# Loads on one queue: a cap on the kilobytes that are underway before the next load is issued

## The chip, the cores and the metric

The kernel runs on one core of one Trainium2 chip. The time is the device time of one execution in microseconds. A core has five engines that run side by side and wait for one another through semaphores: TensorE (PE, with its weight loads shown apart as PEld), VectorE (DVE), ScalarE (ACT), GpSimd (POOL) and SyncE (SP). SP computes nothing here; it issues the DMA transfers between the chip's main memory and the on-chip buffers, one after the other, and 16 DMA engines carry them out.

## The reference

The program is an attention block followed by a gated feed-forward block with a short convolution, over 8 batches of 576 positions, 8 heads of width 64, model width 512 and inner width 1024, all in float32.

```python
scores = scale * np.matmul(q, k.transpose(0, 1, 3, 2))
rel = pos[:, None] - pos[None, :]
mask_plain = (rel >= 0) & (rel < window)                                  # window 32, heads 0 to 3
mask_dil = (rel >= 0) & (rel < window * dilation) & (rel % dilation == 0) # dilation 4, heads 4 to 7
attn = softmax(where(mask, scores, -1e9)); x = attn @ v
...
h = np.maximum(x @ w_in, 0.0)
conv_out = sum over k in 0..2 of conv_w[k] * h shifted by k - 1           # along the sequence
gate = 1.0 / (1.0 + np.exp(-conv_out))
return (h * gate @ w_out)
```

The weights `w_in`, `w_out` and `conv_w` arrive in 64-bit floating point. Every query sees 32 keys, so the attention part needs only narrow bands of the score matrix.

## The kernel before

**Attention.** The work goes batch by batch. A batch has four head pairs: pairs 0 and 1 use the plain window ("p"), pairs 2 and 3 the dilated one ("d"). For each pair SP loads one tile `qk` with queries and keys (592 KB for p, 672 KB for d, line 324) and one tile `v` (384 KB, line 326). There are two `qk` buffers and three `v` buffers, used in turn. PE multiplies queries by keys in blocks of 32 by 64 (L352; where the mask is added by PE, L339 comes first), DVE and ACT do the softmax (L378 to L412), PE multiplies by the values (L423), and ACT and DVE split the result into a high part `xa` (L480) and a rest `xb` (L483), since the products that follow are done on two such parts to keep float32 precision.

**Weights.** A function `weights` loads a slice of `w_in` or `w_out` as 64-bit words (L626) and turns it into a high and a low float32 part, with one ACT step first (L635) and four or more DVE steps after it (L637 to L643, L666, L670); some slices are finished by PE and ACT (L655 to L664). The four `w_in` slices of 1024 KB land in the space that will hold the gates later (`g0early` to `g3early`). The `w_out` slices pass through one buffer `raw`, in two halves of 512 KB where the slice is in `HALVED`.

**Feed-forward.** PE computes x times `w_in` (L549 for the first two batches, L511 later), ACT takes the positive part, DVE and ACT do the convolution and the gate (L563 to L581), PE multiplies by `w_out` (L593), and the result is copied (L605) and stored by SP (L608).

**Order.** A planner class adds every piece of work as a task with an engine, a cost and a due time, walks through them by its own estimate of times, and writes each engine's instructions in the order found. The order is fixed when the program is built; at run time each engine takes its instructions in that order and waits on semaphores where data or a buffer is not ready. The planner also puts matmuls without a use (L707) into PE's gaps in the first part of the program. All loads and nearly all stores stand in one list on SP, so a load that waits holds up all that stand behind it. In that list a load waits for its buffer to come free (for `qk` and `v`, PE's last use of it) and for the transfer that used the same semaphore before it; there are eight such semaphores for DMA, taken in turn, and nothing else limits how many loads are underway.

Of the kernel before, what the change touches and what calls it, by code (L numbers as in the profile page):

```python
# [11 lines left out]
I32 = mybir.dt.int32  # L12
# [7 lines left out]
NP = 4  # L20
NB = 18
W = 64
NV = 6
# [72 lines left out]
class Buffer:  # L96


    def __init__(self, pool, spare=0):

        self.pool, self.spare, self.left, self.end, self.t = pool, spare, 0, 0.0, None


class Task:
    def __init__(self, engine, cost, due, run, after, uses, table):
        self.engine, self.cost, self.due, self.run, self.table = engine, cost, due, run, table
        self.after, self.uses, self.end = [t for t in after if t is not None], list(uses), None
        for b in self.uses:
            b.left += 1


class Planner:
# [110 lines left out]
def attn_moe(ctx: ExitStack, tc: tile.TileContext, qk_p, qk_d, v_p, v_d, w_in, w_out, conv, mask, out):  # L223
    nc = tc.nc
# [25 lines left out]
    plan = Planner()  # L250
# [46 lines left out]
    def queries(p, qk, hd, n):  # L297
# [8 lines left out]
        q0 = 512 + g * 48  # L306
        return [(qk[:, q0 + 16 * i:q0 + 16 * i + 32], key(2 * g + i, 4)) for i in range(2)]

    xs, scored = {}, []

    heads = {}

    def head(b, p, behind=None):


        due = PAIR[b][p]
        kind = p // 2
        qk, v, s = (Buffer(n) for n in ("qk", "v", "s"))
        early = NP * b + p in EARLY or behind is not None
        sc = [Buffer(n) for n in (("mm", "mm", "nn") if early else ("att",))]  # L320
        eased = NP * b + p in EASED
        held = lambda: sorted(s.t for s in sc[:2]) + [sc[2].t] if early else (0, 1, 2)
        n = (S + KP, QD + KD)[kind]
        lq = plan.add("SP", n * 0.00124, 3e3 + NP * b + p if behind else due - EXTRA[32], lambda: nc.sync.dma_start(
            out=qk.t[:, :n], in_=(qk_p, qk_d)[kind][b, p % 2]), uses=[qk])
        lv = plan.add("SP", 0.95, 3e3 + NP * b + p if behind else due - EXTRA[33], lambda: nc.sync.dma_start(
            out=v.t, in_=(v_p, v_d)[kind][b, p % 2]), uses=[v])

        def scores():
            at = held()  # L330
            if eased:

                own = ((0, 1), (2, 3)), ((2, 4),), ((1, 1),)
                if kind == 1:
                    own = ((3, 1), (2, 3)), ((3, 1), (2, 3)), ((4, 1),)
                for bank, runs in enumerate(own):
                    c = 0
                    for i, n in runs:
                        nc.tensor.matmul(banks[:, at[bank], c * W:(c + n) * W].rearrange("p (a k) -> p a k", k=W), ones,  # L339
                                         kinds_sb[:, i, :].unsqueeze(1).to_broadcast([128, n, W]),  # L340
                                         start=c == 0, stop=True, skip_group_check=True)
                        c += n
            order = [4 * t + i for i in range(4) for t in range(4)] + [16, 17]
            if kind == 0:
                order = [a + i for i in range(5) for a, end in RUNS if a + i < end]
            for n in order:
                for hd in range(2):
                    slot, quad = place(p, hd, n)
                    bank, c = (0, slot) if slot < 4 else (2, 0) if slot == 4 else (1, slot - 5)
                    parts = queries(p, qk.t, hd, n)  # L350
                    for i, (q, k) in enumerate(parts):
                        nc.tensor.matmul(banks[quad * 32:quad * 32 + 32, at[bank], c * W:c * W + W], q, k,  # L352
                                         start=i == 0 and not eased, stop=i == len(parts) - 1, skip_group_check=True)

        needs, due = behind or ([], due)
        last = plan.add("PE", (0.71, 0.86)[kind] + (0.5 if eased else 0.0), due, scores, [lq, made, kinds, *needs], [qk, *sc, s], "S")
        if NP * b + p in EARLY and b < 2:
            scored.append(last)
        heads[b, p] = last, lv, v, s, sc, held
# [252 lines left out]
    def weights(src, n, due, pair, summed=False, words=None, halved=False):  # L612

        f = n / 512
        hi, lo = pair
        raw = words or (Buffer("raw") if n > 512 else None)
        r, w = [Buffer("r")] if summed else [], [] if summed or n < 512 else [Buffer("w")]
        u = lambda d=F32: (hi.before if n > 512 else hi).bitcast(d)
        t = lambda d=F32: (w[0].t if w else lo.before if n > 512 else lo).bitcast(d)
        pairs = lambda: (raw[0].t.before if words else raw[0].t if raw else conv_raw)[:, :2 * n].bitcast(I32).rearrange("p (n t) -> p n t", t=2)  # L620
        raw, last = [raw] if raw else [], []
        for at in [slice(0, n // 2), slice(n // 2, n)] if halved else [slice(0, n)]:
            both = lambda at=at: pairs()[:, at]
            low, high = (lambda i=i, both=both: both()[:, :, i] for i in range(2))
            f = (at.stop - at.start) / 512
            part = plan.add("SP", 1.27 * f, due - EXTRA[34], lambda both=both, at=at: nc.sync.dma_start(  # L626
                out=both(), in_=src[:, at].bitcast(I32).rearrange("p (n t) -> p n t", t=2)), uses=raw)

            def step(cost, uses, run, after):
                return plan.add("DVE", 0.16 + cost * f, due + EXTRA[21], run, [after], uses)  # L630

            part = plan.add("ACT", 0.16 + 0.5 * f, due + EXTRA[20], lambda at=at, high=high: nc.scalar.activation(  # L635
                out=u()[:, at], in_=high().bitcast(F32), func=AF.Abs, scale=2.0 ** -112), [part], raw)
            part = step(0.265, [], lambda at=at: nc.vector.tensor_scalar(  # L637
                out=u(I32)[:, at], in0=u(I32)[:, at], scalar1=3, scalar2=None, op0=ALU.logical_shift_left), part)
            part = step(0.53, [*raw, *w], lambda at=at, high=high: nc.vector.scalar_tensor_tensor(  # L639
                out=t(I32)[:, at], in0=high(), scalar=-0x80000000, in1=u(I32)[:, at], op0=ALU.bitwise_and, op1=ALU.bitwise_or), part)  # L640
            part = step(0.265, w, lambda at=at: nc.vector.tensor_scalar(
                out=u(I32)[:, at], in0=t(I32)[:, at], scalar1=-0x800000, scalar2=None, op0=ALU.bitwise_and), part)
            last.append(step(0.53, [*raw, *r], lambda at=at, low=low: nc.vector.scalar_tensor_tensor(  # L643
                out=(r[0].t if summed else u())[:, at], in0=low().bitcast(U32), scalar=-2.0 ** -52 if summed else 2.0 ** -52,
                in1=u()[:, at], op0=ALU.mult, op1=ALU.mult), part))
        f = n / 512

        def step(cost, uses, run):
            return plan.add("DVE", 0.16 + cost * f, due + EXTRA[21], run, list(last), uses)

        if summed:
            part = plan.add("ACT", 0.16 + 0.465 * f, due + EXTRA[22], lambda: nc.scalar.copy(out=hi[:, :], in_=t()), last)

            def add(ps, at):
                nc.tensor.matmul(bank(ps), ident, t()[:, at], start=True, stop=False)  # L655
                nc.tensor.matmul(bank(ps), minus, r[0].t[:, at], start=False, stop=False)
                nc.tensor.matmul(bank(ps), minus, hi[:, at], start=False, stop=True)

            halves, added = [slice(0, 512), slice(512, 1024)], []
            pss = [Buffer("nn" if words else "mm") for _ in halves]  # L660
            for at, ps in zip(halves, pss):
                added.append(plan.add("PE", 1.43, due + EXTRA[23], lambda at=at, ps=ps: add(ps, at), [part, whole, negated], [*r, ps], "E"))

            return [plan.add("ACT", 0.6, due + EXTRA[24], lambda at=at, ps=ps: nc.scalar.copy(out=lo[:, at], in_=bank(ps)), added, [ps])  # L664
                    for at, ps in zip(halves, pss)]
        last = [step(0.53, w, lambda: nc.vector.tensor_tensor(out=t(), in0=t(), in1=u(), op=ALU.add))]  # L666
        if n < 512:
            return last[0]
        last = [plan.add("ACT", 0.16 + 0.465 * f, due + EXTRA[22], lambda: nc.scalar.copy(out=hi[:, :], in_=t()), last, w)]
        return [step(0.53, w, lambda: nc.vector.tensor_tensor(out=lo[:, :], in0=t(), in1=hi[:, :].bitcast(F32), op=ALU.subtract))] * 2  # L670
# [129 lines left out]
```

## Time and profile before

| what | value |
| --- | --- |
| median of 3 runs | 522.52 us (522.17 to 525.08) |
| the profiled execution's own time | 521.72 us |
| its span in the trace | 519.8 us |
| PE busy | 501.5 us (96%) |
| DVE busy | 392.0 us (75%) |
| ACT busy | 289.9 us (56%) |
| chain that ended last | PE 86%, DVE 6%, DMA 3%, issue 2%, ACT 2% |
| bytes on the loads' and stores' queue q1 | 51.10 MB |

The span is what the trace covers; some 1.9 us of the execution lie outside it. The page gives each engine's busy time, the granted TensorE clock and the share of the 16 DMA engines in slices of the span. "Issue" stands for time in which an engine waited for nothing that the profile shows. A row of the timeline has the start in us, the duration, the engine, the line, what was written from what, and in brackets how long the engine stood idle before and what released it. A row on a DMA issue gives the tile, the size, and the time from the issue to the landing of the last byte. The queue q8, of kind "instruction", brings program code: 58 packets and 0.95 MB in all.

### The profile page before, as it was taken

To read this page: it belongs to the slowest core of one execution; us is meant where nothing else is said; L and a number is where in the kernel's file an instruction comes from. 1 tells how busy PE (TensorE), PEld (TensorE's weight loads), DVE (VectorE), ACT (ScalarE), POOL (GpSimd) and SP (SyncE) were. 2 spreads that over 40 slices of the span, in tenths; PEclk is the share of its full clock that TensorE was granted. 3 is DMA by queue.
4 is the path that set the end of the run, shared out by engine and by line. 5 is a ranking of instruction groups with operands and counts; after the bars stand their busy time and mean duration, and the time that the engine had idled before them with its cause. 6 is when DMAs were issued, how large, how long until landed. Compare 5 with 4: busy or idle time off the path is not lost.

```text
span 519.8 us, 16579 instructions
## 1 busy us (share of the span) xinstructions
PE 501.5 (96%) x7416; PEld 438.5 (84%) x7416; DVE 392.0 (75%) x654; ACT 289.9 (56%) x648; POOL 2.0 (0%) x34
## 2 busy tenths in 40 slices
PE   7869999999999899999999999999999999999996
PEld 4547889998888699998888899998788899998885
DVE  3798999999999778799987759887685339982400
ACT  5785788757832258784342248875261258772410
POOL 1000000000000000000000000000000000000000
PEclk9998999999999999999999999999999999999999
DMA  8994551201546610005444700004431100001111
GB/s 290 340 365 149 152 173 54 83 0 42 184 157 212 200 45 0 1 0 184 146 150 137 238 31 1 0 2 135 156 99 45 43 21 0 1 1 42 40 53 50
DMA packets 16695, 52.29 MB, mean 101 GB/s; under 512 B 2032, under 2 KB 2416, under 8 KB 16112
## 3 DMA queue, kind: packets, MB, share of 16 engines
q1 hardware_dynamic: 16480, 51.10, 28.8%
q8 instruction: 58, 0.95, 0.8%
q10 hardware_dynamic: 144, 0.13, 0.1%
q14 instruction: 13, 0.11, 0.1%
HBM read 41.79 MB, written 9.44 MB: 99 GB/s over the span
## 4 chain that ended last, share of the span: by engine, by line
PE 86%; DVE 6%; DMA 3%; issue 2%; ACT 2%; SPq 0%; DVEq 0%; ACTq 0%
PE banks L593 38%; PE banks L511 29%; PE banks L549 6%; PE banks L423 6%; PE banks L352 5%; DMA qk<-in_qk_d_dram 2%; DVE u L563 1%; PE banks L707 1%; DMA qk<-in_qk_p_dram 1%; PE banks L655 1%; ACT s L389 1%; DVE m L378 0%; DVE w L639 0%; DVE x3b L483 0%; DVE r L643 0%
## 5 line engine op out<-in xcount | busy, mean ns | idle before, releaser
L593 PE MATMUL banks<-wo,g 128*128 128x512 f32 x864 | 204.2, 393 | 0.3 <-issue 0.3
L593 PEld LDWEIGHTS banks<-wo,g 128*128 128x128 f32 x864 | 160.3, 188 | 33.6 <-issue 0.5
L563 DVE SCALAR_TENSOR_TENSOR u<-u,conv_sb,u 128x576 f32<-128x576 f32 x104 | 84.3, 817 | 25.6 <-ACT u L569 24.5
L605 ACT COPY u<-banks 128x512 f32<-128x512 f32 (+1 forms) x36 | 20.9, 580 | 81.2 <-PE banks L593 79.8
L524 ACT ACTIVATE u<-banks 128x192 f32<-128x192 f32 (+1 forms) x96 | 36.8, 408 | 27.1 <-PE banks L511 24.8
L511 PE MATMUL banks<-x1a,wi 128*128 128x384 f32 x144 | 48.3, 335 | 0.0
L511 PE MATMUL banks<-x2a,wi 128*128 128x384 f32 x144 | 48.1, 334 | 0.0
L511 PE MATMUL banks<-x0a,wi 128*128 128x384 f32 x144 | 48.0, 335 | 0.0
L511 PE MATMUL banks<-x3a,wi 128*128 128x384 f32 x144 | 48.0, 335 | 0.0
L423 PE MATMUL banks<-pt,v 32*64 32x64 f32 (+2 forms) x2752 | 39.1, 227 | 6.9 <-issue 5.6
L423 PEld LDWEIGHTS banks<-pt,v 32*64 32x64 f32 x2752 | 35.1, 131 | 12.3 <-issue 7.4
L576 DVE TENSOR_TENSOR u<-u,u 128x576 f32<-128x576 f32 x52 | 38.9, 757 | 4.6 <-ACT u L574 4.1
L569 ACT ACTIVATE u<-u,conv_sb 128x576 f32<-128x576 f32 x52 | 40.6, 783 | 0.7
L352 PEld LDWEIGHTS banks<-qk 64*32 64x32 f32 x2432 | 28.7, 105 | 14.3 <-issue 9.0
L574 ACT ACTIVATE u<-u 128x576 f32<-128x576 f32 x52 | 35.1, 683 | 9.5 <-DVE u L563 8.8
L581 DVE TENSOR_TENSOR g<-u,g 128x576 fp32r<-128x576 f32 x52 | 38.3, 753 | 1.9 <-ACT g L579 1.7
L352 PE MATMUL banks<-qk 64*32 64x64 f32 x2432 | 34.5, 224 | 3.9 <-DMA qk<-in_qk_d_dram 1.6
L579 ACT CAST g<-u 128x576 fp32r<-128x576 f32 x52 | 34.5, 680 | 5.2 <-DVE u L576 5.1
L403 ACT ACTIVATE s<-s 128x576 f32<-128x576 f32 x23 | 15.8, 686 | 27.6 <-DVE s L401 27.4
L389 ACT ACTIVATE s<-banks,m 128x64 f32<-128x64 f32 x81 | 24.1, 330 | 6.6 <-DVE m L382 6.6
L511 PEld LDWEIGHTS banks<-x0a,wi 128*128 128x128 f32 x144 | 27.0, 188 | 0.1
L511 PEld LDWEIGHTS banks<-x1a,wi 128*128 128x128 f32 x144 | 27.0, 188 | 0.0
(155 smaller groups left out, 807.8 us busy)
## 6 DMA issues: line engine op xcount, KB each, us to landing
qk<-in_qk_d_dram SPq DMA_DIRECT2D x16, 672.0 KB, 5.1
qk<-in_qk_p_dram SPq DMA_DIRECT2D x16, 592.0 KB, 4.1
out_dram<-u SPq DMA_DIRECT2D x31, 256.0 KB, 2.2
v<-in_v_p_dram SPq DMA_DIRECT2D x16, 384.0 KB, 4.3
v<-in_v_d_dram SPq DMA_DIRECT2D x16, 384.0 KB, 4.7
raw<-in_w_out_dram SPq DMA_DIRECT2D x6, 512.0 KB, 6.8
out_dram<-u SPq DMA_DIRECT2D x9, 128.0 KB, 2.3
g0early<-in_w_in_dram SPq DMA_DIRECT2D x1, 1024.0 KB, 9.5
```

The costliest lines, as they stand in the source:

```text
L352: nc.tensor.matmul(banks[quad * 32:quad * 32 + 32, at[bank], c * W:c * W + W], q, k, start=i == 0 and not eased, stop=i == len(parts) - 1, ...
L423: nc.tensor.matmul(banks[hd * 64:hd * 64 + 64, bank, o:o + n], v.t[quad * 32:quad * 32 + 32, block // 2, block % 2 * 64:block % 2 * 64 + 6 ...
L511: nc.tensor.matmul(out if piece < 2 else out.rearrange("p (a n) -> p a n", a=2), wi[jw][fc // 2][:, fc % 2 * 512 + k * 128:fc % 2 * 512 + ...
L524: lambda h=h, ps=ps, n=n, to=to, at=at: nc.scalar.activation(out=h.t[:, to:to + n], in_=bank(ps)[:, at:at + n], func=AF.Relu), [last], [ps ...
L549: nc.tensor.matmul(bank(ps)[:, 0:HALF], wi[jw][fc // 2][:, fc % 2 * 512 + k * 128:fc % 2 * 512 + k * 128 + 128], x[k].t[jx][:, b % 2, hf * ...
L563: nc.vector.scalar_tensor_tensor(out=body(c[fc]), in0=h[fc].t[:, k:S + k], scalar=conv_sb[:, k, fc:fc + 1], in1=body(c[fc]), op0=ALU.mult, ...
L569: t = plan.add("ACT", 0.777, d, lambda fc=fc: nc.scalar.activation(out=body(c[fc]), in_=body(h[fc]), func=AF.Copy, scale=conv_sb[:, 1, fc: ...
L574: t = plan.add("ACT", 0.686, d + shaped, lambda fc=fc: nc.scalar.activation(out=body(c[fc]), in_=body(c[fc]), func=AF.Sigmoid), [t], [c[fc ...
L576: t = plan.add("DVE", 0.755, d + times, lambda fc=fc: nc.vector.tensor_tensor(out=body(c[fc]), in0=body(c[fc]), in1=body(h[fc]), op=ALU.mu ...
L579: hi = plan.add("ACT", 0.675, d + split, lambda fc=fc: nc.scalar.copy(out=gate(fc, 0), in_=body(c[fc])), [t, *(read[b - 1, fc] if b % 2 el ...
L581: lo = plan.add("DVE", 0.755, d + rest, lambda fc=fc: nc.vector.tensor_tensor(out=gate(fc, 1), in0=body(c[fc]), in1=gate(fc, 0).bitcast(F3 ...
L593: nc.tensor.matmul(bank(ps), g[k].t[:, k % 2, jg, col:col + 128], wo[jw][k // 2][:, k % 2 * 512:k % 2 * 512 + 512], start=(k == 0 and i == ...
```

## The change

Each load of `qk`, `v` and the weights now goes through one helper. It keeps a list of the loads issued so far that are not known to have landed, with their kilobytes. Before it issues a load it drops loads from the front of the list until those left hold at most 1,050 KB, and makes the new load wait for the landing of the last one dropped. The very first load of the masks, and all stores, stay outside the helper. The tasks, their costs, due times and order are the same. The sizes it counts are 592 or 672 KB for `qk`, 384 KB for `v`, 1024 or 512 KB for a weight slice or its half, and 24 KB for the convolution's weights.

```diff
--- before.py
+++ after.py
@@ -107,6 +107,9 @@
         self.after, self.uses, self.end = [t for t in after if t is not None], list(uses), None
         for b in self.uses:
             b.left += 1
+
+
+AHEAD = 1050
 
 
 class Planner:
@@ -306,6 +309,18 @@
         q0 = 512 + g * 48
         return [(qk[:, q0 + 16 * i:q0 + 16 * i + 32], key(2 * g + i, 4)) for i in range(2)]
 
+    underway = []
+
+    def load(to, what, kb):
+
+        it, behind = nc.sync.dma_start(out=to, in_=what), None
+        while sum(k for k, _ in underway) > AHEAD:
+            behind = underway.pop(0)[1]
+        if behind is not None:
+            tc.add_manual_dep(it.ins, behind.ins.name, mybir.DependencyInfo(mybir.DependencyClass.Sync, mybir.DependencyReason.DATA),
+                              reason="few loads underway")
+        underway.append((kb, it))
+
     xs, scored = {}, []
 
     heads = {}
@@ -321,10 +336,10 @@
         eased = NP * b + p in EASED
         held = lambda: sorted(s.t for s in sc[:2]) + [sc[2].t] if early else (0, 1, 2)
         n = (S + KP, QD + KD)[kind]
-        lq = plan.add("SP", n * 0.00124, 3e3 + NP * b + p if behind else due - EXTRA[32], lambda: nc.sync.dma_start(
-            out=qk.t[:, :n], in_=(qk_p, qk_d)[kind][b, p % 2]), uses=[qk])
-        lv = plan.add("SP", 0.95, 3e3 + NP * b + p if behind else due - EXTRA[33], lambda: nc.sync.dma_start(
-            out=v.t, in_=(v_p, v_d)[kind][b, p % 2]), uses=[v])
+        lq = plan.add("SP", n * 0.00124, 3e3 + NP * b + p if behind else due - EXTRA[32], lambda: load(
+            qk.t[:, :n], (qk_p, qk_d)[kind][b, p % 2], n // 2), uses=[qk])
+        lv = plan.add("SP", 0.95, 3e3 + NP * b + p if behind else due - EXTRA[33], lambda: load(
+            v.t, (v_p, v_d)[kind][b, p % 2], NV * 64), uses=[v])
 
         def scores():
             at = held()
@@ -623,8 +638,8 @@
             both = lambda at=at: pairs()[:, at]
             low, high = (lambda i=i, both=both: both()[:, :, i] for i in range(2))
             f = (at.stop - at.start) / 512
-            part = plan.add("SP", 1.27 * f, due - EXTRA[34], lambda both=both, at=at: nc.sync.dma_start(
-                out=both(), in_=src[:, at].bitcast(I32).rearrange("p (n t) -> p n t", t=2)), uses=raw)
+            part = plan.add("SP", 1.27 * f, due - EXTRA[34], lambda both=both, at=at: load(
+                both(), src[:, at].bitcast(I32).rearrange("p (n t) -> p n t", t=2), at.stop - at.start), uses=raw)
 
             def step(cost, uses, run, after):
                 return plan.add("DVE", 0.16 + cost * f, due + EXTRA[21], run, [after], uses)
```

On PE, DVE, ACT and POOL the instructions and their waits are the same as before. On SP the order is the same too; what differs is what a load waits for. A name such as DMAHW3_49 is one of the eight DMA semaphores, and it stands for the landing of the last transfer that used it. They are taken in turn by all transfers on SP: the masks have DMAHW0, the convolution's weights DMAHW1, the first `qk` DMAHW2, and so on.

The first place is the start of SP's list, from the first `v` (DMAHW3) to the second of two halves of a `w_out` slice. Before:

```order
L326 DMA v_90<-in_v_p_dram 128x768
L324 DMA qk_89<-in_qk_d_dram 128x1344
L626 DMA g0early<-in_w_in_dram 128x2048
L324 DMA qk_88<-in_qk_d_dram 128x1344 [waits DMAHW2_49,PE_49]
L626 DMA raw_131<-in_w_out_dram 128x1024
L324 DMA qk_89<-in_qk_d_dram 128x1344 [waits DMAHW4_49,DMAHW0_49,PE_49]
L626 DMA raw_131<-in_w_out_dram 128x1024 [waits DMAHW1_49]
```

And now:

```order
L316 DMA v_90<-in_v_p_dram 128x768
L316 DMA qk_89<-in_qk_d_dram 128x1344
L316 DMA g0early<-in_w_in_dram 128x2048 [waits DMAHW3_49]
L316 DMA qk_88<-in_qk_d_dram 128x1344 [waits DMAHW4_49,DMAHW2_49,PE_49]
L316 DMA raw_131<-in_w_out_dram 128x1024 [waits DMAHW5_49]
L316 DMA qk_89<-in_qk_d_dram 128x1344 [waits DMAHW6_49,DMAHW0_49,PE_49]
L316 DMA raw_131<-in_w_out_dram 128x1024 [waits DMAHW7_49,DMAHW1_49]
```

Nothing moved; `g0early` now waits for the first `v`, the `qk` behind it for the `qk` ahead of it, and each later load here for the one two places ahead.

The second place is some ten loads on, on the same engine, where two `w_in` slices follow each other (`g1early` whole, `g2early` in halves) and the third is near. Before:

```order
L626 DMA g1early<-in_w_in_dram 128x2048
L626 DMA g2early<-in_w_in_dram 128x1024 [waits DMAHW7_49]
L626 DMA g2early<-in_w_in_dram 128x1024 [waits DMAHW0_49]
L324 DMA qk_89<-in_qk_p_dram 128x1184 [waits DMAHW1_49,PE_49]
L326 DMA v_91<-in_v_p_dram 128x768 [waits DMAHW2_49,PE_49]
L626 DMA g3early<-in_w_in_dram 128x2048 [waits DMAHW3_49]
```

And now:

```order
L316 DMA g1early<-in_w_in_dram 128x2048 [waits DMAHW3_49]
L316 DMA g2early<-in_w_in_dram 128x1024 [waits DMAHW5_49]
L316 DMA g2early<-in_w_in_dram 128x1024 [waits DMAHW6_49]
L316 DMA qk_89<-in_qk_p_dram 128x1184 [waits PE_49]
L316 DMA v_91<-in_v_p_dram 128x768 [waits DMAHW0_49,PE_49]
L316 DMA g3early<-in_w_in_dram 128x2048
```

Here `g1early` has taken DMAHW6, so the second half of `g2early` waits for `g1early` to have landed, and the `v` ahead of `g3early` for that second half. Before, these loads waited for transfers that lay eight places back.

## The prediction

> **What bounds the kernel now.** I read the page's head first, then the busy times by stretch (columns: the stretch, its length, busy time and count for PE, PEld, DVE, ACT and POOL, PE's granted clock, DMA share, GB/s).
>
> ```profile
> span 519.8 us, 16579 instructions
> PE 501.5 (96%) x7416; PEld 438.5 (84%) x7416; DVE 392.0 (75%) x654; ACT 289.9 (56%) x648; POOL 2.0 (0%) x34
> 5.00:10.00 5.00, 3.44 (x150) 2.28 (x149) 0.99 (x3) 1.87 (x14) 0.00 (x0) 1.00 0.98 370
> 10.00:15.00 5.00, 4.19 (x129) 2.51 (x112) 3.94 (x9) 3.36 (x18) 0.00 (x0) 1.00 1.01 409
> 35.00:40.00 5.00, 2.35 (x89) 1.85 (x90) 3.47 (x7) 2.65 (x17) 0.00 (x0) 0.89 0.92 330
> 40.00:45.00 5.00, 5.00 (x96) 3.25 (x95) 3.89 (x7) 3.41 (x6) 0.00 (x0) 0.77 0.36 119
> 86.00:516.00 430.00, 426.82 (x5661) 381.22 (x5661) 321.08 (x517) 227.30 (x429) 0.00 (x0) 1.00 0.23 77
> ```
>
> From 86 us on PE is busy 426.8 of 430 us at full clock, while the DMA engines are used 23%. There a load can cost or save little. In the first 40 us it is the other way round: the DMA engines are full (share 0.92 to 1.01) and PE idles (2.35 of 5 us at 35 to 40). So a change to loads is worth what it moves the end of this opening; the rest follows as it stands.
>
> The chain of waits in the opening (start, duration, what):
>
> ```profile
> 7.03 7.19 DMA qk<-in_qk_d_dram
> 14.26 1.13 PE banks L352 x66
> ...
> 18.54 1.38 issue
> ...
> 35.97 2.00 issue
> 37.97 1.30 PE banks L423 x61
> ```
>
> PE waits for a `qk` to 14.22, and stands twice for nothing but "issue", 1.38 and 2.00 us, inside a run of value matmuls. What ends these two? The DMA view of 17.4 to 17.5 and of 35.5 to 35.6 shows one packet each on the instruction queue:
>
> ```profile
> q8 instruction: 1, 0.02, 69.1%
> ```
>
> ```profile
> q8 instruction: 1, 0.02, 61.3%
> ```
>
> PE goes on at 19.92 and 37.97, 2.5 and 2.4 us after them: twice the same distance. So I read them as PE short of code. The page has 58 such packets for 7,416 matmuls and as many weight loads, 256 instructions a packet. PE's waits for "issue" in 0 to 46 us (total, times, longest), and the count of packets:
>
> ```profile
> PE banks L423 <- issue: 3.4, 2, 2.0
> PE banks L352 <- issue: 0.6, 1, 0.6
> q8 instruction: 7, 0.11, 1.0%
> ```
>
> and in 86 to 516 us:
>
> ```profile
> PE banks L423 <- issue: 2.2, 2, 1.5
> PE banks L352 <- issue: 0.5, 1, 0.5
> PE banks L593 <- issue: 0.3, 1, 0.3
> q8 instruction: 44, 0.72, 0.7%
> ```
>
> That is 4.0 us for 7 packets beside full DMA engines, 0.57 each, against 3.0 for 44, 0.07 each. Longer matmuls explain part of the difference, for they use up code more slowly; crowded DMA engines may explain the rest.
>
> **The change, term by term.** No instruction is added to PE, DVE or ACT. SP gains waits, and behind each stand all later loads, though no store in the opening. To see when loads land now, I take the time from issue to landing of loads that ran alone (in order: at 45, 98.7, 48.6, 85 and 67.6 us):
>
> ```profile
> v<-in_v_p_dram SPq DMA_DIRECT2D x1, 384.0 KB, 3.4
> raw<-in_w_out_dram SPq DMA_DIRECT2D x1, 512.0 KB, 3.5
> qk<-in_qk_p_dram SPq DMA_DIRECT2D x1, 592.0 KB, 3.8
> qk<-in_qk_d_dram SPq DMA_DIRECT2D x1, 672.0 KB, 4.4
> raw<-in_w_out_dram SPq DMA_DIRECT2D x1, 1024.0 KB, 4.8
> ```
>
> Full engines move 409 GB/s (the row at 10 to 15), so 2.56 us for 1,024 KB. A load then lands at the later of two times: its issue plus its time alone, or the landing ahead of it plus its share of 2.56 us. The start, as issued and as it landed among others:
>
> ```profile
> 2.11 0.43 SPq L326 DMA_DIRECT2D v<-in_v_p_dram  x1
> 2.58 0.43 SPq L324 DMA_DIRECT2D qk<-in_qk_d_dram  x1
> g0early<-in_w_in_dram SPq DMA_DIRECT2D x1, 1024.0 KB, 9.5
> qk<-in_qk_d_dram SPq DMA_DIRECT2D x1, 672.0 KB, 6.7
> v<-in_v_p_dram SPq DMA_DIRECT2D x1, 384.0 KB, 4.8
> ```
>
> The `v` lands at 6.9 (2.11 + 4.8), and `g0early`, which was issued at about 3.06 (9.5 before it landed, just ahead of 12.57), waits for that. The `qk` between them lands at 8.6 (6.9 + 1.68, alone) to 9.3 (2.58 + 6.7, as before). Then, issue and landing: `g0early` 6.95, 11.8; `qk` 9.0, 13.6; `raw` 11.85, 15.35; `qk` 13.65, 18.05; `raw` 15.4, 19.3; `v` 18.1, 21.5; `qk` 18.5, 23.0; `v` 19.4, 24.0; `v` 21.55, 25.0; `g1early` 23.05, 27.9; the halves of `g2early` 25.05, 29.2 and 27.95, 31.45. Further on the same way: `v` 31.5, 34.9; `g3early` 31.9, 37.5; `v` 37.55, 41.0; the last `raw` half 41.05, 44.55. Where these are used now:
>
> ```profile
> 12.57 1.13 ACT L635 ACTIVATE wi03early<-g0early 128x1024 f32<-128x1024 f32 x1 [1.64 <-DMA g0early<-in_w_in_dram]
> 28.77 1.22 ACT L635 ACTIVATE wi02early<-g1early 128x1024 f32<-128x1024 f32 x1
> 30.76 1.35 ACT L635 ACTIVATE wi00early<-g2early 128x512 f32<-128x512 f32 x2
> 33.59 0.70 ACT L480 CAST x2a<-banks 128x64 fp32r<-128x64 f32 x2 [0.32 <-PE banks L423]
> 34.77 0.68 DVE L483 TENSOR_TENSOR x2b<-banks,x2a 128x512 fp32r<-128x512 f32 x1
> 45.69 0.68 ACT L635 ACTIVATE wo02early<-raw 128x512 f32<-128x512 f32 x1
> 50.03 0.41 ACT L556 ACTIVATE u<-banks 128x288 f32<-128x288 f32 x1 [3.66 <-PE banks L549]
> ```
>
> *First term, the early loads.* `g0early` and the third `qk` come about 0.7 us sooner (11.8 for 12.55, 13.6 for the 14.22 of the chain), because nothing is queued behind them that shares the engines. Both are waited for, so ACT and PE start sooner by 0.6. But the second half of `g2early`, at 31.45, then holds ACT: 0.68 for its L635 (half of 1.35) and 1.16 for the step behind it (L652, from 32.11 to 33.27, where the 0.32 idle begins) put L480 at 33.29 instead of 33.59. So at most 0.3 reaches DVE at 34.77. I take -0.3; the other bound is 0 (the loads share the engines as before). A shorter first stall (1.38) would be stopped at the same place, so it is worth nothing more.
>
> *Second term, the stall at 35.97.* It is ended by the code packet, not by PE's own work, so what counts is how soon that packet gets through. The loads that stood before it, first and last of five:
>
> ```profile
> 27.37 0.47 SPq L626 DMA_DIRECT2D g3early<-in_w_in_dram  x1
> 34.49 0.37 SPq L626 DMA_DIRECT2D raw<-in_w_out_dram  x1
> ```
>
> With their sizes they are 1024 + 512 + 384 + 672 + 512 = 3,104 KB, of which `g3early` was nearly through. By the list above only the `v` of 31.5 and `g3early` are underway at 34, 1,408 KB. Nothing in this trace shows the packet's time with half the queue. Bounds are 0 (it comes no sooner) and -2.0 (the stall goes); I take the middle, -1.0, since the 0.57 against 0.07 us a packet says crowding matters, and since the packet ahead of it came late too and would now come sooner.
>
> *Third term, lateness behind.* Loads land up to 2.5 us later from 19 to 45 us. The last `raw`, 44.55, is in time for ACT at 45.69, though only just if ACT is 1 us sooner; ACT has 3.66 us idle behind that row, so I count 0. After 45 us loads are far enough apart that the wait is met when SP comes to it, but for a few that are wanted only much later: 0.
>
> Sum: 519.8 - 0.3 - 1.0 = 518.5 of span, 520.4 of execution (521.72 - 1.3). The median of the runs lies 0.8 above that execution, so 522.52 - 1.3 = **521.2 us**.
>
> **Rivals.**
>
> *Code comes no sooner* (chance 0.24). The stalls shrink only if packets on q8 wait behind queued loads. If the engines serve q8 in turn with q1, depth does not matter, and only the first term stays: 522.52 - 0.3 = 522.2. Against it are the 0.57 us a packet; for it, that value matmuls outran their code by 1.5 us in the late stretch too, where the DMA engines are used 23%. The Trainium skill, "DMA: Bandwidth & Descriptors", section on queues, rings and completion order, says that each DMA engine goes round the queue rows it has work for, a packet at a time; by that rule this rival holds. Our two packets beside full engines do not settle it.
>
> *The whole stall goes, and the clock stays up* (0.15). PE's gaps of 34 to 38 us are followed by a clock of 0.77 in 40 to 45, with PE busy throughout: 5 x 0.23 = 1.2 us lost. Without the stall both come back: -0.3 - 2.0 - 1.2 = -3.5, 519.0 us. DVE and ACT must follow: ACT idles 2.35 of 5 us and DVE 1.53 at 35 to 40, so they could.
>
> *The waits starve the engines* (0.16). Each hand-off (landing, wait, issue, first byte) leaves the DMA engines with little queued. If each costs 0.4 us more than my list, five follow one another up to `g2early`'s second half, which lands at 33.45. DVE's x2b follows ACT's L480, which follows that landing by 1.84; x2b itself comes 0.7 after L480's start, so at 35.99 instead of 34.77. That is +1.2, 523.7 us. It decides from a landing of 32.2 on; a loss of 0.5% needs 34.8.
>
> *The waits never bind* (0.02): each is met before SP comes to it, 522.5 us. Against it: `g0early` stood ready to issue at 3.06, 3.8 us ahead of the landing it must now wait for.
>
> **How the numbers follow.** The forecast has 0.43. I count as no change what is within 0.5% (2.6 us), about what a measurement of this kernel can tell. Its own range is 520.2 to 522.5 by the bounds of the second term. With the rivals at 519.0 and 523.7 on the two ends, 519.0 to 523.8 holds 8 in 10. Faster by over 0.5%, below 519.9: the third of the cases nearly whole, 0.13, and 0.08 of the forecast's where the clock recovers too: 0.21. Slower, above 525.1: the far end of the starving case and things unseen, 0.11. Within: 0.68.
>
> **What would show it.** `g0early` used by ACT near 11.9 and PE's third score block near 13.6 show the first term; the first later than 12.6 refutes it. An "issue" gap near 35 us of 1 us is the second term; 2 us is the first rival, none with the clock at 1.00 the second. ACT's wait for a half of `g2early` above 1 us is the starving case. PE's busy share from 86 us on must stay as it is; a new wait for a load there would make all of this wrong.

## The result: slower by 1.05%, and the profile after

| | before | changed |
| --- | --- | --- |
| median, timed side by side | 523.24 us (4 runs, 522.17 to 525.08) | 528.73 us (4 runs, 527.58 to 530.66) |
| ratio, with its 95% interval | | 1.0105 (1.0061 to 1.0149) |
| the profiled execution | 521.72 us, span 519.8 | 527.58 us, span 525.5 |

Executions that fell into a slower state of the chip are left out of the times here and below. The forecast was 521.2 us, with a range of 519.0 to 523.8. The changed kernel lies outside it, on the other side. The page's head and the busy times by stretch of the changed kernel (the same columns as in the prediction):

```profile
span 525.5 us, 16579 instructions
5.00:10.00 5.00, 3.84 (x165) 2.73 (x165) 1.28 (x4) 2.58 (x18) 0.00 (x0) 1.00 0.91 332
10.00:15.00 5.00, 2.88 (x17) 1.31 (x15) 2.86 (x8) 2.27 (x10) 0.00 (x0) 1.00 0.77 257
30.00:35.00 5.00, 1.29 (x73) 1.12 (x72) 2.47 (x4) 2.65 (x4) 0.00 (x0) 0.68 0.75 225
35.00:40.00 5.00, 3.84 (x139) 3.20 (x132) 3.55 (x7) 3.70 (x15) 0.00 (x0) 0.50 0.89 333
40.00:45.00 5.00, 5.00 (x79) 3.20 (x63) 4.92 (x9) 3.04 (x11) 0.00 (x0) 0.50 0.70 220
86.00:516.00 430.00, 426.88 (x5735) 381.72 (x5734) 325.53 (x523) 230.70 (x436) 0.00 (x0) 1.00 0.23 76
```

In the last row PE is as busy as before, to 0.06 us of 430. One ACT instruction at the end of the opening, before and changed, shows where the time went:

```profile
86.86 0.81 ACT L569 ACTIVATE u<-u,conv_sb 128x576 f32<-128x576 f32 x1
```

```profile
91.21 0.81 ACT L584 ACTIVATE u<-u,conv_sb 128x576 f32<-128x576 f32 x1
```

By then the changed kernel is 4.35 us behind, of the 5.7 us by which its span is longer. So most of the time went in the opening, as the prediction said it could only go there; where the other 1.3 us of this one execution went is not settled here. What differs is the DMA side of the opening: a share of 0.77 and 257 GB/s at 10 to 15 us, where it was 1.01 and 409. PE is busy 1.29 of 5 us at 30 to 35, and behind that its clock is 0.50 for ten microseconds.

The chain of waits in the changed kernel (start, duration, what):

```profile
8.84 6.26 DMA qk<-in_qk_d_dram
...
15.18 4.85 DMA qk<-in_qk_d_dram
...
20.43 5.12 DMA qk<-in_qk_p_dram
...
25.57 6.47 DMA g1early<-in_w_in_dram
...
32.05 4.22 DMA g2early<-in_w_in_dram
...
36.71 6.79 DMA g3early<-in_w_in_dram
...
49.05 3.60 DMA raw<-in_w_out_dram
```

Each of these is one load from its issue to its landing, and each landing is what the next waits for: 15.10, 20.03, 25.55, 32.04, 36.27, 43.50, and 52.65 for the last half of `raw`. SP and the loads have become the chain; no computing engine stands between. Before, two loads stood in it, to 14.2 us, and then none to 132 us; from 23 to 60 us it was mostly steps on DVE and ACT, with PE at 36 to 43:

```profile
1.64 4.32 DMA qk<-in_qk_p_dram
...
7.03 7.19 DMA qk<-in_qk_d_dram
...
25.89 2.47 ACT s L389 x16
...
33.64 1.22 DVE w L639
...
132.39 5.33 DMA qk<-in_qk_d_dram
```

Where ACT uses the loads in the changed kernel:

```profile
13.50 1.12 ACT L650 ACTIVATE wi03early<-g0early 128x1024 f32<-128x1024 f32 x1 [2.73 <-DMA g0early<-in_w_in_dram]
32.06 1.12 ACT L650 ACTIVATE wi02early<-g1early 128x1024 f32<-128x1024 f32 x1 [3.54 <-DMA g1early<-in_w_in_dram]
34.02 0.69 ACT L650 ACTIVATE wi00early<-g2early 128x512 f32<-128x512 f32 x1
36.30 0.69 ACT L650 ACTIVATE wi00early<-g2early 128x512 f32<-128x512 f32 x1 [1.59 <-DMA g2early<-in_w_in_dram]
52.67 0.68 ACT L650 ACTIVATE wo02early<-raw 128x512 f32<-128x512 f32 x1 [4.11 <-DMA raw<-in_w_out_dram]
```

These are the rows L635 of before, 15 lines further down. `g0early` is used 0.93 us later than before (13.50 for 12.57), `g1early` 3.29 later (32.06 for 28.77), the last `raw` 6.98 later (52.67 for 45.69). The idle times in brackets are waits for the DMA; of these loads only `g0early` had one before, 1.64 us. The wait of 3.54 for `g1early` passes on to PE, as its longest of the whole trace. Beside it the waits for "issue" (total, times, longest):

```profile
PE banks L354 <- ACT wi L679: 4.2, 1, 4.2
PE banks L438 <- issue: 2.1, 2, 1.5
PE banks L367 <- issue: 1.1, 2, 0.6
```

The same view of before, over its whole span, for "issue":

```profile
PE banks L423 <- issue: 5.6, 4, 2.0
PE banks L352 <- issue: 1.4, 3, 0.6
PE banks L593 <- issue: 0.3, 1, 0.3
```

So 7.3 us of "issue" became 3.2. The waits that the prediction hoped to shorten are shorter by 4.1 us, but nothing shows that any time was won by it: in the opening, where they went, PE now stands for loads and for the other engines instead.

The whole stretch from 5 to 45 us sums it up. Before, then changed:

```profile
5.00:45.00 40.00, 31.44 (x906) 20.20 (x904) 29.99 (x63) 27.17 (x114) 0.00 (x0) 0.96 0.88 328
```

```profile
5.00:45.00 40.00, 30.61 (x815) 19.95 (x814) 29.03 (x61) 25.41 (x113) 0.00 (x0) 0.83 0.82 279
```

328 GB/s fell to 279. That is 49 GB/s x 40 us = 1.96 MB less brought in. At 328 GB/s it takes 6.0 us to make up, which is near the 5.5 us lost, but the nearness is no rule: of the caps below, the same sum gives 4.6 us for the 3.6 lost at 1,500 KB, and 20 us for the 48 lost at 0.

### The profile page after: what moved, and what is told of

It is laid out like the page before. It is cut to its first block, busy times and chain, and to the rows that moved or that the text cites. A ratio compares the mean times of both kernels' runs of the same rounds, so it can differ in the third digit from the quotient of the medians.

```text
span 525.5 us, 16579 instructions
## 1 busy us (share of the span) xinstructions
PE 504.7 (96%) x7416; PEld 441.2 (84%) x7416; DVE 392.6 (75%) x654; ACT 289.7 (55%) x648; POOL 2.0 (0%) x34
## 4 chain that ended last, share of the span: by engine, by line
PE 84%; DMA 11%; DVE 2%; issue 1%; ACT 1%; SPq 0%; DVEq 0%
PE banks L608 38%; PE banks L526 29%; PE banks L564 7%; PE banks L438 5%; PE banks L367 5%; DMA qk<-in_qk_d_dram 3%; DMA qk<-in_qk_p_dram 3%; DMA g3early<-in_w_in_dram 1%; DMA g1early<-in_w_in_dram 1%; DMA v<-in_v_d_dram 1%; DVE u L578 1%; DMA g2early<-in_w_in_dram 1%; DMA raw<-in_w_out_dram 1%; SPq L316 0%; DVE u L591 0%
## 5 line engine op out<-in xcount | busy, mean ns | idle before, releaser
L526 PEld LDWEIGHTS banks<-x3a,wi 128*128 128x128 f32 x144 | 27.3, 190 | 0.0
```

The lines of the kernel that those rows point to most:

```text
L526: nc.tensor.matmul(out if piece < 2 else out.rearrange("p (a n) -> p a n", a=2), wi[jw][fc // 2][:, fc % 2 * 512 + k * 128:fc % 2 * 512 + ...
```

## Experiments

Each kernel is compared with the kernel before on the same chip. Edits are shown against the changed kernel unless it says otherwise. Letters of theories are those of the quoted text. In it, a load's number counts the transfers on SP's queue: the 27th is the `qk` behind the last `raw` and two `v`, and the 28th the `qk` behind that.

### Where the loss is

The cap for the first 23 loads through the helper only, up to the last half of `raw`:

```diff
-    underway = []
+    underway, issued = [], []
...
+        issued.append(it)
+        if len(issued) > 23:
+            behind = None
```

> The cap of 1,050 KB holds for the 23 loads of the opening (up to the last raw half near 45 us) and for none behind them. Theory A, the opening's hand-offs starve the DMA engines: the whole loss stays, +4 to +6 us against before. Rival B, waits behind 45 us cost: +3 us at most, as the change shows a shift of +3.2 us near 50 us and +4.4 near 58 us.

Measured: 528.06 us, ratio 1.0107 (1.006 to 1.0154). The whole loss is there, within the interval. In its profiled execution, of 529.76 us, the ACT row of 86.86 comes at 95.86, so 9.0 us late, where it was 4.35 late in the changed kernel's. The first 23 loads and their waits are the same in both. So the cost of the opening differs by some microseconds from one execution to the next, and a single profile tells where the time goes better than how much. The complement has `<= 23` in place of `> 23`:

> The first 23 loads are free as before, the cap holds behind them. Theory A: no loss, within 0.6 us of before. Rival B: +2 to +3 us.

Measured: 521.89 us, ratio 1.0001 (0.998 to 1.0022). The waits of all later loads cost nothing that shows, which the prediction had counted so. From here on only the first 23 loads matter.

### How the loss goes with the cap

```diff
-AHEAD = 1050
+AHEAD = 2100
```

> The cap doubled to 2,100 KB. Theory A: a hand-off now finds two loads queued, the engines stay fed, and loads land within 1 us of before; the time is -1 to +1 us of before, a gain only if PE's waits for code near 18 and 36 us shrink as they did with the cap at 1,050 KB. Rival C, the loss comes from any added wait on SP, whatever is queued: +3 us or more.

> The cap at 1,500 KB, between. Theory A: part of the loss, +1 to +3 us, g1early landing between 28.4 us (before) and 32.0 us (the change). Rival D, the loss is the clock that falls to 0.5 after PE's gap of 4.2 us: near 0 if the gap stays under 3 us, even where loads land 2 us late.

At the other end one load at a time, `AHEAD = 0`:

> A cap of 0 KB: each load waits until the one before it has landed. Theory A: every load of the opening takes its time alone (3.4 to 4.8 us, the sum of 24 near 100 us), so the opening ends 45 to 60 us later, and PE's waits for code in it shrink to below 1 us, since a code packet finds the queue empty. If code packets stay 2 us or more late even so, crowding by loads was not what delayed them.

| cap, KB | time, us | ratio (95% interval) | GB/s, 5 to 45 us | DMA share | last `raw` used by ACT, us |
| --- | --- | --- | --- | --- | --- |
| none | (compared with) | 1 | 328 | 0.88 | 45.69 |
| 2,100 | 523.51 | 1.0032 (1.0015 to 1.005) | 327 | 0.90 | 44.99 |
| 1,500 | 525.90 | 1.0062 (1.0035 to 1.009) | 290 | 0.82 | 49.33 |
| 1,050 | 528.73 | 1.0105 (1.0061 to 1.0149) | 279 | 0.82 | 52.67 |
| 0 | 570.38 (one run) | 1.09 (one run by 522.24) | 160 | 0.48 | 85.99 |

The smaller the cap, the fewer bytes arrive in the opening and the longer the time. At 2,100 KB the profiled opening brings as much as before and its last `raw` is no later. The 0.3% that remains there is not explained by this column: the profiled execution, of 521.06 us, is the quickest of the twelve and does not have that loss. By the medians (522.33 for before) the cap of 2,100 costs 1.2 us and that of 1,500 costs 3.6, each a little more than theory A left for it; rival C's 3 us for any added wait did not come at 2,100. The run at 1,500 does not part theory A from rival D. Its longest gap of PE in the opening is 2.9 us, under the 3 us that D asked for, but the clock fell all the same, to a mean of 0.83 over 5 to 45 us.

With a cap of 0 the kernel is 48 us slower, where 45 to 60 were expected. PE has no wait for "issue" in its first 62 us, but that does not tell whether code came sooner, since PE stands for loads there, up to 9.7 us at a time.

The kernel with a cap of 0 also shows what a load costs that is truly alone. The DMA issues in 0 to 60 us (tile, size, median us from issue to landing), with a cap of 0:

```profile
g0early<-in_w_in_dram SPq DMA_DIRECT2D x1, 1024.0 KB, 4.7
g1early<-in_w_in_dram SPq DMA_DIRECT2D x1, 1024.0 KB, 4.8
g2early<-in_w_in_dram SPq DMA_DIRECT2D x2, 512.0 KB, 3.7
```

and the same loads in the changed kernel:

```profile
g0early<-in_w_in_dram SPq DMA_DIRECT2D x1, 1024.0 KB, 6.7
g1early<-in_w_in_dram SPq DMA_DIRECT2D x1, 1024.0 KB, 6.5
g2early<-in_w_in_dram SPq DMA_DIRECT2D x2, 512.0 KB, 4.0
```

The 4.8 us that the prediction took for 1,024 KB is right for a load with nothing beside it. With a cap of 1,050 KB there is something beside it: the load behind, which is issued while this one still runs. `g0early` lands at 13.48, just ahead of its use, so it is issued near 6.76 (6.7 before), the `qk` behind it at 8.84 (the chain above), 4.6 us before `g0early` lands. The two are underway together, and the first of them lands at 13.48 in place of 11.5. The second lands at 15.10. At the full rate its share of 1.68 us behind 13.48 would make 15.16, but that this fits is chance, since the engines were far from full in between:

```profile
13.50:14.00 0.50, 0.00 (x0) 0.00 (x0) 0.00 (x0) 0.50 (x1) 0.00 (x0) 1.00 0.29 118
14.00:14.50 0.50, 0.00 (x0) 0.00 (x0) 0.00 (x0) 0.50 (x1) 0.00 (x0) 1.00 0.40 65
14.50:15.00 0.50, 0.00 (x0) 0.00 (x0) 0.34 (x1) 0.50 (x4) 0.00 (x0) 1.00 0.87 224
```

That is 0.2 MB in 1.5 us, so most of the 672 KB had come before. The load that waited for `g0early`, a `raw`, was issued at 13.50, and the rate is back above 200 GB/s only a microsecond later.

### Which waits

Only one load waits, `g0early`, the fifth through the helper:

```diff
+        issued.append(it)
+        if len(issued) != 5:
+            behind = None
```

> One added wait only: g0early waits for the first v, as in the change; nothing else does. Theory A, a wait is harmless while other loads stand behind it: g0early lands by 12.6 us, g1early near 28.5 us, and the time is within 0.6 us of before. Rival E: g0early lands at 13.5 us as in the change and the time is +1 us.

Measured: 523.13 us, ratio 1.0031 (1.001 to 1.0052). One wait costs 0.9 us by the medians (522.24 for before) and 1.6 by the ratio, more than the 0.6 that theory A left for it. Rival E's time came, but not its landing: ACT uses `g0early` at 13.04, between the 12.57 of before and the 13.50 of the change. PE's clock is 0.66 at 15 to 20 us with PE busy throughout, and no run tells how much of the cost is that; the "issue" stall near 37 us is still there, 2.0 us.

The `w_in` slices never wait, all other loads do (the flag is set for them alone):

```diff
+        if free:
+            behind = None
```

> The change, but the five loads of w_in slices never wait for the cap; all others do. Theory A: g0early lands near 11.5 us and g1early near 29 us instead of 32.0, the gap of 4.2 us in PE near 30 us shrinks to about 1 us, and half of the loss or more is gone (+1 to +2.5 us). Rival E, every added wait costs its own 1 us whichever load it holds: the loss falls only by the four of about twenty waits of the opening that are gone, +4 us or more.

and the opposite, `if not free`, where only the `w_in` slices wait:

> The other half of the run in which the w_in slices were free: now only the loads of w_in slices (five, with the two halves) wait by the cap, and qk, v and raw do not. If the costs of the waits add up, the loss is what that run left out, 1.05 - 0.54 = 0.5%, near 525 us. If it is one chain of hand-offs that must be closed to cost (each load waiting for the one ahead), breaking it at either half takes away more than half: within 0.3% of before, 522 to 523.8 us. If waits of large loads alone cost, all of it stays: 528 us.

Measured: 524.42 us, 1.0054 (1.003 to 1.0079), and 523.94 us, 1.0033 (0.9999 to 1.0067). The two halves make 0.87% together, the whole 1.05%, with intervals of 0.25 to 0.45% to either side: they may add up, and neither half carries it all. The 523.94 of the second lies between what its text gives for one chain (up to 523.8) and for costs that add up (near 525), and does not part the two. The first is 2.2 us slower than before, as theory A had it, and not the 4 of rival E. But while `g0early` came at 11.68, `g1early` was used at 32.05 as in the changed kernel, not near 29 as theory A had it: it stands in SP's list behind loads that wait. Being free helps a load little when the list ahead of it is not free.

### Is it PE's clock?

In the changed kernel PE's clock falls to 0.50 behind the 4.2 us gap. A first run has 22 more filling matmuls in the gaps:

```diff
+        longer = []
+        for i, (x, run) in enumerate(sorted(more, key=lambda x: x[0])):
+            longer += [(x, run)] * (1 + {25: 8, 51: 14}.get(i, 0))
```

> The change with 22 more matmuls without a use on PE, 8 and 14 of them behind those that stand ahead of its two long gaps near 13 and 30 us, so that PE is busy while it waits. No load and no wait differs. Theory A, late loads alone: the time stays at +5 us against before, and ACT's steps on the weight slices keep their times. Rival D, the fallen clock: PE's clock in 35 to 45 us stays near 1.00 instead of 0.50, and 1.5 to 3 us of the 5.5 come back.

Measured, beside the changed kernel's 528.73: 543.48 us, ratio 1.0412 (1.0367 to 1.0458). It told nothing of the clock, since PE then stood for "issue" eleven times, 3.85 us at 34.56 the longest and most of the others between 143 and 387 us. That is a finding of its own, followed up below. A second run has 128 small matmuls in the 4.2 us gap alone; with their weight loads these are exactly one packet of 256 instructions, so that behind them every packet ends where it did:

```diff
...
+            longer += [(x, lambda i=i: fill(i))] + [(x, lambda i=i: fill(i, 32, 64))] * {51: 128}.get(n, 0)
...
+        if m < 128:
+            return nc.tensor.matmul(banks[0:m, i, 0:n], ones[:, 0:m], ones[:, 0:n], start=True, stop=True)
```

> The changed kernel with 128 small matmuls of no use (128*32, 64 columns) after the filling matmul at 28.88 us, in the gap of 4.22 us in which PE waits for the low part of g1early. 128 pairs are one whole packet of code, so behind them every border of code falls where it did. They take 4 to 4.5 us if each takes the 34 to 38 ns of the small ones in the run with 112. Rival D (the clock): PE's clock of 0.68, 0.50 and 0.50 in 30 to 45 us is what costs; PE is busy 8.84 us of 35 to 45 at half clock, so up to 4.4 us come back: about 524.5 us, and the 28th load is issued near 55. Theory A (late loads hold the opening whatever the clock): the clock is near 1.00 from 30 to 45, but PE, ACT and DVE wait longer for the second half of g2early (36.3), for g3early (43.5) and the last raw (52.7), which do not come sooner; 28th load within 1 us of 59.3, 527.7 to 529 us.

Measured: 528.16 us, ratio 1.0123 (1.0083 to 1.0164). Its stretches, and two of PE's waits in 0 to 62 us:

```profile
30.00:35.00 5.00, 3.74 (x121) 3.52 (x117) 2.46 (x5) 1.52 (x3) 0.00 (x0) 1.00 0.59 213
35.00:40.00 5.00, 3.00 (x165) 2.49 (x164) 2.44 (x5) 2.93 (x7) 0.00 (x0) 1.00 0.76 242
40.00:45.00 5.00, 3.69 (x91) 2.59 (x92) 4.46 (x9) 3.78 (x21) 0.00 (x0) 0.60 0.88 315
```

```profile
PE banks L441 <- DVE x2b L501: 3.2, 1, 3.2
PE banks L357 <- ACT wi L682: 1.4, 1, 1.4
```

The clock is 1.00 through 40 us (0.60 in the five behind), and nothing is won: PE now stands 3.2 us for `x2b`, which waits for the late `g2early` by way of ACT. The time is theory A's (527.7 to 529 expected), and rival D's 524.5 lies outside the interval. So the low clock is not what costs the 5.5 us. That it costs nothing is not shown: in this execution the second half of `g2early` was used at 38.21, where it was 36.30 in the changed kernel's, and a microsecond or two that the clock gave back could hide behind that.

### What the spoiled run had found

PE's code comes in packets of 256 instructions, by the prediction's count of 58 packets for 7,416 matmuls and as many weight loads. If PE stands where a packet ends inside a run of small value matmuls, a few more pairs of instructions ahead of it move every such place. Four kernels, without the cap unless it says so, edits against the kernel before:

```diff
...
+            longer += [(x, lambda i=i: fill(i))] + [(x, lambda i=i: fill(i, 32, 64))] * {7: 20}.get(n, 0)
```

> The kernel before, without the cap, with 20 small matmuls of no use (64*32, 64 columns, some 15 ns each by the 72 of 0.97 us at 6.00) after the eighth filling matmul, in PE's gap ahead of 6.0 us. Theory C (code borders): packets of code hold 256 instructions, 128 pairs of weight load and matmul, and 20 pairs more move every border 20 pairs back in the program. Laid over the trace of before, with a packet asked for about 44 pairs ahead of the border before it is needed and 3.5 us from asking to use, this puts borders into runs of value matmuls: stalls of 1 to 1.9 us at 33, 140, 165, 173, 234, 251, 270, 286, 295, 367 and 393 us, 18.5 us in all in place of 3.9, so about 522.3 + 14 = 536 us. Rival M: it was the work of the useless matmuls in the run with 22 of them, or the clock, that cost time; then these 0.3 us in a gap cost nothing: 522 us, within 1.

Measured: 539.59 us, ratio 1.0325 (1.0268 to 1.0382). Twenty matmuls of some 35 ns, in a gap, cost 17 us. PE's waits for "issue" in this kernel:

```profile
PE banks L426 <- issue: 14.0, 8, 3.2
PE banks L355 <- issue: 2.8, 2, 2.3
PE banks L596 <- issue: 1.2, 2, 0.7
```

18.0 us, where it was 7.3. These 10.7 us are the larger part of the 15.0 by which this profiled execution (536.74) is slower; the rest is not traced. The stalls stand where theory C laid them: the first four of over 1 us behind 30 us begin at 32.6, 140.3, 167.4 and 176.3 us, for 33, 140, 165 and 173. Then 112 of them (`{7: 40, 13: 36, 25: 36}`), and 8 filling matmuls fewer:

> The kernel before, without the cap, with 112 such small matmuls (40, 36 and 36 of them after the 8th, 14th and 26th filling matmul, ahead of 6.0, 9.4 and 14.3 us). Theory C: 112 pairs move the borders almost a whole packet, which is the same as 16 pairs forward; laid over the trace the stalls are 0.3 us in all in place of 3.9: 522.3 - 3.6 = 518.7 us, a little more or less by what becomes of the stalls in the opening. Rival M: more matmuls cost more; 112 of them cost over five times what 20 do, and at the least nothing: 522 us or above.

> The kernel before, without the cap, with 8 of the 44 filling matmuls left out (numbers 0, 1, 8, 9 and 14 to 17). Theory C: borders move 8 pairs forward, stalls laid over the trace sum to about 0: 522.3 - 3.9 = 518.4 us, if the gaps where the 8 stood, up to 1 us each, leave the clock as it is. Rival M: filling matmuls left out cost clock, so 522.5 to 525 us.

Measured: 524.73 us, 1.0039 (1.0007 to 1.0071), and 522.82 us, 1.0009 (0.9987 to 1.0032). That over five times as many cost an eighth as much rules out the matmuls themselves, rival M. But the gain that theory C expected did not come: the waits for "issue" are still 6.6 and 6.5 us, at other places. Laying shifted borders over the old trace told the bad places and no better ones. Last, the 8 fewer together with the cap:

> The changed kernel, cap of 1,050 KB, with the same 8 filling matmuls left out. Theory A (the cap's loss lies in late loads of the opening) and theory C together: the late stalls go as without the cap, the loss of the opening stays: the time is e11's plus 4.5 to 6.5 us, about 524 us. If the loss of the cap were itself the borders of code (another number of stalls in the opening or behind it), the two kernels with 8 fewer would lie within 1 us of each other.

Measured: 529.48 us, ratio 1.0115 (1.0066 to 1.0164), 6.7 us above its twin without the cap by the medians, and 1.06% (5.5 us) by the ratios. So the cap's loss stays when the borders lie 8 pairs elsewhere. No kernel among these beats the one before.

## Why the prediction was wrong, step by step

**What bounds the kernel.** Right in where a loss could come: in the opening, while the rest is PE and did not change (busy 426.88 of 430 us). Too broad in calling the first 40 us full of loads with PE idle. One stretch of before that the prediction does not show:

```profile
20.00:25.00 5.00, 5.00 (x115) 3.11 (x115) 3.16 (x9) 2.20 (x4) 0.00 (x0) 1.00 0.77 283
```

Here PE is busy throughout and the DMA engines are at 0.77, and the chain of before has no load from 14.3 us on. The loads of the opening had slack. The cap first used that up, and then what came later than the slack cost time.

**The rule for landings, and with it the first term, -0.3.** This is the step that failed. It took a load as landing after its time alone, or at the full rate behind the load ahead, "because nothing is queued behind them that shares the engines". Something was behind: the cap lets the next load start before a load lands, 2 to 4 us behind the start of a large one, and the loads of 1,024 KB then took 6.5 to 6.8 us in place of 4.8. Nor were the engines full: behind a landing the load that has waited for it must first be issued and begin to move, as at 13.5 to 14.5 us above. `g0early` came at 13.48 for 11.8, and 12.6 had been named as the point that refutes the term. How much of the lateness is the longer loads and how much the holes behind landings, no run parts. As each landing starts the next load, the errors add up:

| load | predicted landing | measured |
| --- | --- | --- |
| `g0early` | 11.8 | 13.48 |
| third `qk` | 13.6 | 15.10 |
| `qk` ahead of `g1early` | 23.0 | 25.55 |
| `g1early` | 27.9 | 32.04 |
| `g2early`, second half | 31.45 | 36.27 |
| `g3early` | 37.5 | 43.50 |
| last `raw` | 44.55 | 52.65 |

The list has its own warning: it brings the last `raw` 2.5 us later than before and calls that harmless.

Another hole just behind a landing, in the changed kernel's busy times by half a microsecond:

```profile
32.00:32.50 0.50, 0.00 (x0) 0.00 (x0) 0.00 (x0) 0.44 (x1) 0.00 (x0) 0.50 0.82 336
32.50:33.00 0.50, 0.00 (x0) 0.00 (x0) 0.00 (x0) 0.50 (x1) 0.00 (x0) 0.50 0.09 33
33.00:33.50 0.50, 0.00 (x0) 0.00 (x0) 0.29 (x1) 0.50 (x2) 0.00 (x0) 0.50 0.90 197
```

`g1early` has landed at 32.04 and the next load was issued at 32.05; half a microsecond later the engines have next to nothing to do, 0.09 and 33 GB/s. With 2,100 KB underway their share over 5 to 45 us is 0.90, with 1,050 it is 0.82.

**The second term, -1.0.** The stall went, but not by the way that the term took, and no time is shown to be won by it. Waits for "issue" fell from 4.0 us to none in the opening, and stayed near 3 behind 86 us (3.0 and 2.7). At the place of the stall of 35.97, PE's runs of value matmuls, before and then changed, and the packet of code at 37.0 to 37.1 us in the changed kernel:

```profile
35.65 0.32 PE L423 MATMUL banks<-pt,v 32*64 32x64 f32 x2 [1.38 <-DVE x2b L483]
```

```profile
39.43 0.92 PE L438 MATMUL banks<-pt,v 32*64 32x64 f32 x37 [1.16 <-DVE x2b L498]
q8 instruction: 1, 0.02, 58.9%
```

The packet came 1.5 us later than the one of 35.5 us before, and PE, held by `x2b`, came to the place 3.8 us later, some 2.4 us behind the packet: the distance at which PE had gone on before. So the stall went because PE fell back further than its code did. Whether the code came sooner after it was asked for, no run shows. So the rival "code comes no sooner", and the rule of the Trainium skill beside it ("DMA: Bandwidth & Descriptors", the section on queues, rings and completion order), are neither shown nor refuted.

**The third term, 0.** Right for loads behind the first 23 (1.0001), wrong for those inside it: the last `raw` at 52.65 is 8 us later than listed, far more than ACT's 3.66 us of slack. The `qk` that waited for it landed at 58.14, and PE stood 1.1 us for that. An ACT row of 53.51 before comes 2.8 us later in the changed kernel, at 56.27, and that of 56.82 comes 4.4 us later, at 61.20.

**The rivals.** The starving case came nearest, at a chance of 0.16 and with 0.4 us a hand-off. Measured are 4.8 us over the same five (36.27 for 31.45), about 1.0 each. Its sign that ACT waits more than 1 us for a half of `g2early` was there (1.59), and its point for a loss of 0.5%, a landing of 34.8, was passed by 1.5 us. With the landing that was measured its own formula gives 36.27 + 1.84 + 0.7 = 38.8 for `x2b` in place of 34.77, and 38.55 is measured. So the mechanism was right, and the path as far as `x2b`; that the last loads would cost again behind it was not in it. The price of 0.4 us a hand-off was taken from nothing in the trace and was less than half of what came. The case of the clock that stays up could not come: behind a 4.2 us gap it fell further.

## What to carry to other kernels

Where the DMA engines are full, the depth of the queue is what keeps them full: over 5 to 45 us they moved 328 GB/s without a cap, and 327, 290, 279 and 160 with 2,100, 1,500, 1,050 and 0 KB. Price a cap by when each load lands and how much slack its use has, and not by the missing bytes alone, which hit the loss in one case here and missed it in the others. The time of a load alone, read in a quiet stretch, is too short to plan with where the next load starts before this one lands (6.5 to 6.8 us for 4.8). And count a wait in a list of loads for the whole list behind it: freeing the `w_in` loads gained about half, and `g1early` came no sooner, since it stood behind loads that waited.

## What was not expected of the hardware

Code. Twenty useless matmuls of some 35 ns made this kernel 3.25% slower (2.68 to 3.82), and PE's waits for "issue" went from 7.3 to 18.0 us; 112 made it 0.39% slower, and 128, a whole packet's worth, left the changed kernel where it was (1.0123 for 1.0105). So where the packets of 256 instructions end was worth up to 17 us among these kernels, with their runs of small matmuls, and an edit that adds a few instructions early on is timed together with that.

The clock. Behind a gap of 4.2 us it was 0.50 for over ten microseconds; in the kernel where only `g0early` waits, a gap of 1.9 us was followed by 0.66 at 15 to 20 us:

```profile
15.00:20.00 5.00, 5.00 (x124) 2.50 (x104) 4.89 (x10) 4.98 (x32) 0.00 (x0) 0.66 1.01 380
```

In the changed kernel a gap of 2.27 us at the same place, ahead of 15.15, was followed by 1.00 at 15 to 20 us. So the length of a gap alone did not decide here.
